# Queueing operations of four small chains one step later in a Fourier, gated and feed-forward kernel

## The chip, the cores and the metric

The kernel runs on one core of a Trainium2 chip. The engines of the core work side by side, each through its own queue in order: TensorE (PE in the profile; PEld is its load of weights), VectorE (DVE), ScalarE (ACT), GpSimd (POOL) and SyncE (SP), which here only issues DMAs. The metric is the device time of one execution in microseconds.

## The reference

Three parts follow one another over `x` of 4 x 3072 x 256:

```python
X = np.fft.rfft(x, axis=1)
Yr = Xr @ w_r - Xi @ w_i + b_r
Yi = Xr @ w_i + Xi @ w_r + b_i
Yr = np.sign(Yr) * np.maximum(np.abs(Yr) - 0.01, 0.0)   # and Yi alike: the soft threshold
x = np.fft.irfft(Yr + 1j * Yi, n=3072, axis=1)

xk = mu_k * x + (1.0 - mu_k) * x_prev                   # x_prev: one token earlier
xr = mu_r * x + (1.0 - mu_r) * x_prev
k = np.maximum(xk @ w_k, 0.0)                           # 256 -> 1024
x = sigmoid(xr @ w_r) * (k * k @ w_v)                   # 1024 -> 256

h = x @ w_in                                            # 256 -> 2048
g = h * np.clip(h + 3.0, 0.0, 6.0) / 6.0
out = g @ w_out                                         # 2048 -> 256
```

The weights of the second and third part come as 64-bit floats.

## The kernel before

Every product is made of three matmuls on fp32r pairs (`three`, L150): high by high, low by high, high by low. The pair of a value is made by `split` (L145): ACT rounds it into the high part, DVE subtracts that for the low part. So nearly each matmul waits for a chain that goes from ACT to DVE.

PE, ACT, DVE and POOL run in the order in which the program emits their instructions (`manual_schedule`, L228); no scheduler moves them. Generators lay the order out: a `yield` ends a *step*, and the loops at the end call the steps of several generators in turn. DMAs are issued from SP in emission order too, the tables of the transforms from POOL.

**The transforms.** The Fourier transform of a batch has a first stage (`s1`, 8 steps per batch, through `sc_a` in DRAM), a middle (`mid`, 12 pairs of groups, through `sc_b`) and an end (`ib`, 8 steps, into `sc_y`). A step of `mid` holds `s2` (12 matmuls, and the split `Xh`, `Xl`), then `mix` (24 matmuls with `w_r` and `w_i`, the bias added at L361, the soft threshold in L362 and L363, on DVE), and `ia` (6 matmuls), whose inputs `yh`, `yl` are split by `split_y` (L366) one step after. `ends` holds the last two pairs of `mid`.

**The weights' decode.** `Weights.load` brings 128x512 64-bit floats from DRAM; `decode` (L184) makes an fp32 value of the two 32-bit halves. L196 takes the exponent out on DVE, L197 and L198 build the power of two on ACT, L200 to L202 put sign and mantissa together on DVE, L204 multiplies, L210 splits. `decoder` (L212) runs jobs staggered: a new job each second step, and on each step one further step of each running job, so three jobs stand at different points of the chain. Buffers for the loaded halves come in threes (`stw`, `stt`).

**The order of the stages.** `first` (L451) is batch 0's transform as far as two `ib` steps, with the decode of `wr`, `wk`, `wv` on the steps named in `DECODE` (L33). Then come 24 tiles of 512 tokens of the second part, five units each (L834): `r`, then `k` four times; the product with `w_v` (`u_v`) follows two units later. At each half unit a slot lets `ahead` (L862) make a step of `prep` for the next tile: `xf` on ACT, `xf` on DVE, the split `kh`, `kl`, twice over (for `xk` and `xr`). Between these units stand the steps of `later` (L453), the transforms of the rest (`feed`), until they run out at some 795 us; from there on the decode of `w_in` and `w_out` (`jobs2`, 16 jobs, 36 decoder steps) takes their place (`decode_to`, L855).

**The third part** runs over 24 tiles with 8 units each (L922). Tile 0 uses plain products (`u_i`, L593). In its units 3 to 7 `beside` also makes the sums of the weights (`sums`, L616, in four quarters c0 to c3) and of tile 1's tokens (`split_s`, L648) that Strassen's products want; tiles 1 to 23 use these (`u_s`, L682), and what is left of the sums (`aside`) goes into tile 1's units. The output product of a unit (`u_o`, 24 matmuls) is issued two units later, in three parts between the matmuls of `u_s` (`cut`, L696). Before the first `u_s` the PSUM pool of the stages before is closed and another one opened (L949).

Of the kernel before, what the change touches and what calls it, by code (L numbers as in the profile page):

```python
# [103 lines left out]
def fourier_mix_ffn_kernel(  # L104
# [54 lines left out]
    class Weights:  # L159
# [24 lines left out]
        def decode(self, staged, k, q, c, m):  # L184
            w, t = staged
            yield
            hi, lo = self.hi[:, k : k + q, c : c + m], self.lo[:, k : k + q, c : c + m]
            if self.wide:
                w = w.rearrange("p k (n s) -> p k n s", s=2)
                low, high = w[:, :, :, 0], w[:, :, :, 1]  # L190
                a = t[:, 0].rearrange("p (k n) -> p k n", k=q)
                f = t[:, 1].rearrange("p (k n) -> p k n", k=q)
                ai, au = a.bitcast(I32), a.bitcast(U32)
                ts, stt = nc.vector.tensor_scalar, nc.vector.scalar_tensor_tensor

                ts(au, high, 20, 0x7FF, op0=ALU.logical_shift_right, op1=ALU.bitwise_and)  # L196
                nc.scalar.activation(f, ai, AF.Relu, bias=top[:, 0], scale=-1.0)  # L197
                nc.scalar.activation(ai, f, AF.Relu, bias=top[:, 1], scale=-(2.0**23))  # L198
                yield
                stt(au, high, 0x80000000, au, op0=ALU.bitwise_and, op1=ALU.bitwise_or)  # L200
                ts(high, high, 0xFFFFF, 0x100000, op0=ALU.bitwise_and, op1=ALU.bitwise_or)
                stt(f, low, 2.0**-32, high, op0=ALU.mult, op1=ALU.add)  # L202
                yield
                nc.vector.tensor_mul(f, f, a)  # L204
            else:
                f = w
                yield
                yield
            yield
            split(f, hi, lo)  # L210

    def decoder(jobs, stage):  # L212

        running = []
        for n in range(2 * len(jobs) + 4):
            for r in running:
                next(r, None)
            running = running[-3:]
            if n % 2 == 0 and n // 2 < len(jobs):
                w, *job = jobs[n // 2]  # L220
                running.append(w.decode(w.load(stage, *job), *job))
            yield
# [5 lines left out]
    with tc.manual_schedule(engines=order):  # L228
# [7 lines left out]
        omu = cst.tile([128, 2, 2], F32, name="omu")  # L236
        half = cst.tile([128, 1], F32, name="half")
        top = cst.tile([128, 2, 1], F32, name="top")
        bias = fp.tile([128, 3, D], F32, name="bias")
# [38 lines left out]
        def fetch():  # L278

            split_chunks(head["use"] + 4)  # L280
            load_chunks(head["split"] + 4)
# [31 lines left out]
        def mid(b):  # L313
# [31 lines left out]
            def mix(j):  # L345
# [13 lines left out]
                yl = fp.tile([128, 512], F32R, tag="yl", bufs=2, name="yl")  # L359
                bs = bias[:, 0:2] if j == 0 else bias[:, 1:3]  # L360
                nc.vector.tensor_add(y, p[:, 0:512], bs.rearrange("p g d -> p (g d)"))  # L361
                nc.vector.tensor_scalar(m, y, LAM, 0.0, op0=ALU.add, op1=ALU.min)  # L362
                nc.vector.scalar_tensor_tensor(y, y, LAM, m, op0=ALU.subtract, op1=ALU.max)  # L363
                yy[j] = (y, yh, yl)

            def split_y(j):  # L366
# [3 lines left out]
            def ia(j):  # L370
# [8 lines left out]
                nc.sync.dma_start(out=gb[j], in_=sb[:, 0:2])  # L379

            for j in range(NP + 1):
                if j < NP:
                    s2(j)
                load_t(b, j + 2)
                if j >= 2:
                    split_y(j - 2)
                if j < NP:
                    yield
                if j:
                    mix(j - 1)  # L390
                    fetch()
                    yield
                if 2 <= j < NP:
                    ia(j - 2)

            def end(j):
# [70 lines left out]
        nc.vector.memset(zero, 0.0)  # L467
        nc.vector.memset(half, 0.5)
        nc.vector.memset(top[:, 0], 1170.0)
        nc.vector.memset(top[:, 1], 254 * 2.0**23)  # L470

        def vectors():
# [4 lines left out]
            with nc.allow_non_contiguous_dma(reason="two vectors"):  # L477
                for i, m in enumerate((mu_k, mu_r)):
                    nc.sync.dma_start(out=mus[:, i], in_=m.rearrange("(a p) -> p a", p=128))
            nc.vector.tensor_scalar(omu, mus, -1.0, 1.0, op0=ALU.mult, op1=ALU.add)  # L480


# [9 lines left out]
        def prep(i):  # L492
# [9 lines left out]
            for w in (1, 0):  # L502
# [13 lines left out]
                l = kb.tile([128, 2, TOK], F32R, tag="kl", bufs=3, name="kl")  # L516
                nc.scalar.activation(h, xf, AF.Copy)  # L517
                nc.vector.tensor_sub(l, xf, h.bitcast(F32))  # L518
                xs[i, w] = h, l
# [72 lines left out]

        def u_i(i, j):  # L593
            xh, xl = xt[i]
# [11 lines left out]
            nc.vector.scalar_tensor_tensor(g, g, 1.0, p, op0=ALU.min, op1=ALU.mult)  # L606
            split(g, h, l)
            hg[i, j] = (h, l)
# [73 lines left out]
        def u_s(sp, pz, i, j, other, before, aside):  # L682
# [12 lines left out]
            c11, c21 = cc[:, 0:256], cc[:, 256:512]  # L695
            cut = [len(other) * n // 3 for n in range(4)]  # L696

# [130 lines left out]
        preps = prep(0)  # L828
        for _ in range(3):
            next(preps)  # L830
            next(preps)
            next(fs)

# [18 lines left out]

        done2 = 0

        def decode_to(n):  # L855
# [6 lines left out]
        def ahead(i, slot):  # L862

            nonlocal preps
            if i + 1 == len(seq):
# [8 lines left out]
            if slot == late and i + 1 < len(seq):  # L874
                b, t = seq[i + 1]
                drain(b, (TOK * t + TOK - 1) // N1 // 4 if t else 0)
                load_y(i + 1)
                preps = prep(i + 1)
            elif slot >= late + 2:
                next(preps, None)  # L880

        for n, (i, kind, j) in enumerate(units):
# [19 lines left out]
            if not live_f:  # L902
                if jobs2 is None:
# [13 lines left out]
                    jobs2 = decoder(wi.jobs + wo.jobs, stage2)  # L917
                decode_to(36 * (n - n0 + 1) // (len(units) - n0))
        units = [(i, j) for i in range(len(tiles)) for j in range(8)]
        pend = []  # L920
        before = []
        for n, (i, j) in enumerate(units):  # L922
            if i == 0:
                decode_to(max(done2 + 2, 2 * (j // 2 * 2 + 1) + 6, 2 * (8 + j) + 6))
                u_i(i, j)
                if lag:
# [3 lines left out]
                elif j > 2:  # L930
                    for f in u_o(*pend.pop(0)):
                        f()
                if j == 3:
                    decode_to(len(wi.jobs + wo.jobs) * 2 + 4)
                    stage.close()
                    sp = ctx.enter_context(tc.tile_pool(name="sp", bufs=1))
                    sw = [sp.tile([128, 4, 8, 128], F32R, name=f"sw{c}") for c in range(2)]
                    c0, c1, c2, c3 = (sums(sp, c) for c in range(4))
                    x1 = split_s(sp, 1)
                    beside = {3: c0[:2], 4: c0[2:] + c1[:1], 5: c1[1:], 6: x1[:2], 7: x1[2:] + c2[:1]}  # L940
                    aside = c2[1:] + c3
                if j >= 3:
                    for on_vector, on_scalar in beside[j]:
                        on_vector()
                        if on_scalar:
                            on_scalar()
            else:
# [38 lines left out]
```

## Time and profile before

| | us |
|---|---|
| median of three runs | 2081.03 (2080.89 to 2084.46) |
| the profiled execution | 2082.47 |
| its span | 2080.7 |
| PE busy | 1992.8 (96%) |
| PE's weight loads busy | 1844.5 (89%) |
| DVE busy | 1549.8 (74%) |
| ACT busy | 1323.2 (64%) |

The granted clock of TensorE was 0.976 of full speed over the span. A busy time says in how much of the span an engine worked on something; the stages differ, so the stretches between the stages' borders are read one by one. 0 to 40 us is the first stage of batch 0, 40 to 125 its middle, 125 to 195 the rest of `first` and the first tile's start, 195 to 795 the second part beside the transforms, 795 to 1052 the second part beside the decode, 1052 to 1120 tile 0 of the third part and the passage to tile 1, and 1120 to the end the Strassen tiles.

### The profile page before, as it was taken

The page shows a single profiled execution, that of the slowest core. Times are in us where ns is not written, and L with a number is a line of the kernel's source. Part 1 is how long each engine was busy: PE and PEld are TensorE (multiplying, and loading weights), DVE is VectorE, ACT ScalarE, POOL GpSimd, SP SyncE. Part 2 cuts the span into 40 slices and gives each one's busy share as a digit, 9 for nine tenths or more (in the row PEclk, how much of TensorE's full clock was granted, in tenths as well). Part 3 has the DMA queues.
Part 4 walks back from the last instruction along what each step waited for, and adds up shares of the span by engine and source line. Part 5 has one row for each costly group of instructions (what it writes and reads, how often), then busy time and mean ns, then how long its engine had stood idle before and what let it go on. Part 6 is the DMA issues. An engine that isn't in the chain of part 4 may idle for free.

```text
span 2080.7 us, 33798 instructions
## 1 busy us (share of the span) xinstructions
PE 1992.8 (96%) x13928; PEld 1844.5 (89%) x13928; DVE 1549.8 (74%) x1975; ACT 1323.2 (64%) x1917; POOL 35.0 (2%) x63
## 2 busy tenths in 40 slices
PE   6878999999999999889998999999999999999998
PEld 4867998898789888667787999999999999999998
DVE  3868667777677686767777777877787778777875
ACT  5556447555754565555646777777777777667775
POOL 0000000000000000000000000000000000000000
PEclk7978999999999999999999999999999999999999
DMA  9765447543653352122100001100110011001100
GB/s 265 240 205 165 123 114 228 163 142 115 216 170 111 95 179 65 63 75 77 51 31 24 29 23 29 32 21 23 30 32 21 22 31 32 21 22 31 32 11 21
DMA packets 106988, 175.85 MB, mean 85 GB/s; under 512 B 12945, under 2 KB 63314, under 8 KB 106834
## 3 DMA queue, kind: packets, MB, share of 16 engines
q1 hardware_dynamic: 96034, 141.76, 22.1%
q0 software_dynamic: 10480, 31.67, 5.7%
q8 instruction: 109, 1.79, 0.4%
q14 instruction: 45, 0.37, 0.1%
q10 hardware_dynamic: 320, 0.26, 0.0%
HBM read 110.35 MB, written 63.31 MB: 83 GB/s over the span
## 4 chain that ended last, share of the span: by engine, by line
PE 76%; DVE 14%; ACT 6%; issue 2%; DMA 2%; SPq 0%; ACTq 0%; DVEq 0%
PE oacc L776 24%; PE rq L776 15%; PE acc L156 8%; PE pk L156 7%; PE cc L776 6%; PE mix L156 5%; PE s L156 4%; DVE g L552 2%; DVE gl L553 2%; PE pr L156 2%; DVE xf L511 1%; PE ia L156 1%; DVE kl L518 1%; PE ib L421 1%; PE ib L420 1%
## 5 line engine op out<-in xcount | busy, mean ns | idle before, releaser
L776 PE MATMUL oacc<-wo_hi,gl 128*128 128x256 f32 x1536 | 426.7, 278 | 0.6 <-DVE gl L750 0.6
L776 PE MATMUL oacc<-wo_hi,gh 128*128 128x256 f32 x1536 | 427.1, 278 | 0.0
L776 PE MATMUL oacc<-wo_lo,gh 128*128 128x256 f32 x1536 | 425.4, 277 | 0.0
L776 PEld LDWEIGHTS oacc<-wo_hi,gl 128*128 128x128 f32 x1536 | 288.7, 188 | 1.0 <-DVE gl L750 0.8
L776 PEld LDWEIGHTS oacc<-wo_hi,gh 128*128 128x128 f32 x1536 | 288.5, 188 | 0.2
L776 PEld LDWEIGHTS oacc<-wo_lo,gh 128*128 128x128 f32 x1536 | 288.7, 188 | 0.0
L732 DVE TENSOR_TENSOR c<-rq,s 128x512 f32<-128x512 f32 x184 | 127.3, 692 | 184.2 <-ACT s L728 184.2
L745 DVE SCALAR_TENSOR_TENSOR g<-g,c 128x1024 f32<-128x1024 f32 x184 | 225.5, 1226 | 27.1 <-ACT g L744 17.4
L749 ACT ACTIVATE gh<-g 128x1024 fp32r<-128x1024 f32 x184 | 195.2, 1061 | 55.8 <-DVE g L745 55.8
L750 DVE TENSOR_TENSOR gl<-g,gh 128x1024 fp32r<-128x1024 f32 x184 | 223.7, 1216 | 1.2 <-ACT gh L749 1.2
L776 PE MATMUL rq<-th,sw 128*128 128x256 f32 x1104 | 217.4, 277 | 7.3 <-DVE g L606 7.3
L744 ACT ACTIVATE g<-c,half 128x1024 f32<-128x1024 f32 x184 | 211.5, 1150 | 4.1 <-DVE c L733 1.4
L712 ACT ACTIVATE s<-rq 128x512 f32<-128x512 f32 x184 | 109.9, 598 | 112.0 <-PE rq L776 111.5
L776 PEld LDWEIGHTS rq<-th,sw 128*128 128x128 f32 x1104 | 166.4, 188 | 7.5 <-DVE g L606 7.5
L156 PE MATMUL acc<-gl,wv_hi 128*128 128x512 f32 x384 | 153.8, 400 | 13.3 <-DVE gl L553 13.3
L547 ACT ACTIVATE g<-pk 128x1024 f32<-128x1024 f32 x96 | 97.6, 1016 | 106.5 <-PE pk L156 106.4
L156 PE MATMUL pk<-kh,wk_hi 128*128 128x512 f32 x384 | 152.8, 398 | 9.3 <-ACT kh L517 5.2
L776 PE MATMUL rq<-tl,sw 128*128 128x256 f32 x552 | 153.9, 279 | 2.8 <-DVE tl L679 2.8
L148 DVE TENSOR_TENSOR al<-a,ah 96x512 fp32r<-96x512 f32 (+1 forms) x176 | 114.9, 684 | 55.2 <-ACT ah L147 55.2
L156 PE MATMUL acc<-gh,wv_hi 128*128 128x512 f32 x384 | 153.2, 399 | 1.6 <-ACT gh L551 1.5
L156 PE MATMUL acc<-gh,wv_lo 128*128 128x512 f32 x384 | 152.2, 396 | 0.0
L156 PE MATMUL pk<-kl,wk_hi 128*128 128x512 f32 x384 | 151.9, 396 | 0.0
(150 smaller groups left out, 4953.0 us busy)
## 6 DMA issues: line engine op xcount, KB each, us to landing
tt<-in_tab_dram POOLq DMA_DIRECT2D x40, 640.0 KB, 4.9
yt<-sc_y SPq DMA_DIRECT2D x23, 608.0 KB, 3.9
a<-in_x_dram SPq DMA_DIRECT2D x64, 192.0 KB, 3.5
sc_a<-s1sb SPq DMA_DIRECT2D x32, 384.0 KB, 3.9
a<-sc_a SPq DMA_DIRECT2D x48, 256.0 KB, 3.2
sc_b<-iasb SPq DMA_DIRECT2D x48, 256.0 KB, 4.8
a<-sc_b SPq DMA_DIRECT2D x64, 192.0 KB, 3.1
sc_y<-ysb SPq DMA_DIRECT2D x32, 384.0 KB, 2.9
```

The costliest lines, as they stand in the source:

```text
L148: nc.vector.tensor_sub(l, src, h.bitcast(F32))
L156: nc.tensor.matmul(o, a, c, start=first and i == 0, stop=last and i == n - 1, **kw)
L547: nc.scalar.activation(g, p, AF.Relu)
L552: nc.vector.tensor_mul(g, g, g)
L553: nc.vector.tensor_sub(l, g, h.bitcast(F32))
L712: nc.scalar.activation(s[:, 1:3].rearrange("p a n -> p (a n)"), rq, AF.Copy)
L732: nc.vector.tensor_add(c[:, 1::2], two(rq), s[:, 0:2])
L744: nc.scalar.activation(g, c, AF.Relu, bias=half, scale=1.0 / 6.0)
L745: nc.vector.scalar_tensor_tensor(g, g, 1.0, c, op0=ALU.min, op1=ALU.mult)
L749: lambda: nc.scalar.activation(h, g, AF.Copy),
L750: lambda: nc.vector.tensor_sub(l, g, h.bitcast(F32)),
L776: return lambda: nc.tensor.matmul(o, lhs, rhs, start=start, stop=stop, skip_group_check=True)
```

## The change

Four chains are cut at other places into steps; three of them keep their instructions.

- *Decode.* The `yield` stands after L196 instead of after L198, L204 follows L202 without one, and the two halves of the split at L210 are steps of their own. A job takes six steps behind its load instead of five, and `decoder` runs one step more.
- *Tiles' inputs.* In `prep` the low part `kl` is a step of its own, eight steps instead of six per tile. `ahead` spreads those that are left over the slots that are left, and the loop ahead of the units makes all eight for tile 0.
- *Soft threshold.* `bias` is lowered by `LAM` once (768 columns, on DVE, in `vectors`). `mix` is a generator now: it adds the bias, then after `fetch` an activation on ACT makes relu(-y - 2 `LAM`) with the column `lam2` as its bias, and at the top of the next pair DVE takes the maximum of y and minus that. The operation at L362 goes.
- *Sums and tile 0.* Tile 1's sums (`x1`) come first, from unit 3 on, and what `u_i` gets as `between` is emitted between the unit's rounding copy and its low part. c0 and c1 up to its rounding copy stay in tile 0; c1's low part, all of c2 and c3 go to tile 1 (`aside`). The decode is finished ahead of `u_i` of unit 3, not behind it, and the first `u_s` issues all of `u_o`'s 24 matmuls ahead of its own.

```diff
@@ Weights.decode
                 ts(au, high, 20, 0x7FF, op0=ALU.logical_shift_right, op1=ALU.bitwise_and)
+                yield
                 nc.scalar.activation(f, ai, AF.Relu, bias=top[:, 0], scale=-1.0)
                 nc.scalar.activation(ai, f, AF.Relu, bias=top[:, 1], scale=-(2.0**23))
                 yield
...
                 stt(f, low, 2.0**-32, high, op0=ALU.mult, op1=ALU.add)
-                yield
                 nc.vector.tensor_mul(f, f, a)
...
             yield
-            split(f, hi, lo)
+            nc.scalar.activation(hi, f, AF.Copy)
+            yield
+            nc.vector.tensor_sub(lo, f, hi.bitcast(F32))
@@ decoder
-        for n in range(2 * len(jobs) + 4):
+        for n in range(2 * len(jobs) + 5):
@@ mix
                 nc.vector.tensor_add(y, p[:, 0:512], bs.rearrange("p g d -> p (g d)"))
-                nc.vector.tensor_scalar(m, y, LAM, 0.0, op0=ALU.add, op1=ALU.min)
-                nc.vector.scalar_tensor_tensor(y, y, LAM, m, op0=ALU.subtract, op1=ALU.max)
                 yy[j] = (y, yh, yl)
+                yield
+                nc.scalar.activation(m, y, AF.Relu, bias=lam2, scale=-1.0)
+                yield
+                nc.vector.scalar_tensor_tensor(y, m, -1.0, y, op0=ALU.mult, op1=ALU.max)
@@ mid
+            rest = iter(())
             for j in range(NP + 1):
+                next(rest, None)
                 if j < NP:
                     s2(j)
...
                 if j:
-                    mix(j - 1)
+                    rest = mix(j - 1)
+                    next(rest)
                     fetch()
+                    next(rest)
                     yield
...
+            next(rest, None)
@@ constants and vectors
+        nc.vector.memset(lam2, -2 * LAM)
...
+            nc.vector.tensor_scalar(bias, bias, LAM, None, op0=ALU.subtract)
@@ prep
                 nc.scalar.activation(h, xf, AF.Copy)
+                yield
                 nc.vector.tensor_sub(l, xf, h.bitcast(F32))
@@ u_i
-            split(g, h, l)
+            nc.scalar.activation(h, g, AF.Copy)
+            for f in between:
+                f()
+            nc.vector.tensor_sub(l, g, h.bitcast(F32))
@@ u_s
-            cut = [len(other) * n // 3 for n in range(4)]
+            cut = [len(other) * n // 3 for n in range(4)] if (i, j) > (1, 0) else [0, 0, 0, 0]
+            if (i, j) == (1, 0):
+                for f in other:
+                    f()
@@ before the units' loop
-        for _ in range(3):
+        for n in range(4):
             next(preps)
             next(preps)
-            next(fs)
+            if n < 3:
+                next(fs)
@@ ahead
                 preps = prep(i + 1)
+                left = 8
             elif slot >= late + 2:
-                next(preps, None)
+                for _ in range(-(-left // (10 - slot))):
+                    next(preps, None)
+                    left -= 1
@@ the second part's loop
-                decode_to(max(done2 + 2, 2 * (j // 2 * 2 + 1) + 6, 2 * (8 + j) + 6))
-                u_i(i, j)
+                decode_to(max(done2 + 2, 2 * (j // 2 * 2 + 1) + 7, 2 * (8 + j) + 7))
+                if j == 3:
+                    decode_to(len(wi.jobs + wo.jobs) * 2 + 5)
...
+                    x1 = split_s(sp, 1)
+
+                    beside = {
+                        3: ([x1[0][0]], [x1[0][1]]),
+                        4: ([x1[1][0]], [x1[1][1], c0[0][0]]),
+                        5: ([x1[2][0]], [c0[1][0]]),
+                        6: ([c1[0][0]], [c0[1][1], c0[2][0]]),
+                        7: ([c1[1][0]], [c1[1][1]]),
+                    }
+                    both = lambda f, g: lambda: (f(), g())
+                    aside = [(both(c1[2][0], c2[0][0]), None), c2[1], (both(c2[2][0], c3[0][0]), None)] + c3[1:]
+                u_i(i, j, beside[j][0] if j >= 3 else ())
                 if lag:
...
-                if j == 3:
-                    decode_to(len(wi.jobs + wo.jobs) * 2 + 4)
...
-                    beside = {3: c0[:2], 4: c0[2:] + c1[:1], 5: c1[1:], 6: x1[:2], 7: x1[2:] + c2[:1]}
-                    aside = c2[1:] + c3
                 if j >= 3:
-                    for on_vector, on_scalar in beside[j]:
-                        on_vector()
-                        if on_scalar:
-                            on_scalar()
+                    for f in beside[j][1]:
+                        f()
```

## Rows read from the trace of the kernel before

**Rows 1.** Windows by stage: stretch, us, busy us (instructions) of PE, PEld, DVE, ACT, POOL, PEclk, DMA, GB/s.
```profile
40.00:125.00 85.00, 71.31 (x522) 67.15 (x522) 69.44 (x114) 44.15 (x72) 8.63 (x14) 0.92 0.76 230
125.00:195.00 70.00, 54.86 (x244) 46.06 (x245) 47.92 (x80) 48.90 (x84) 0.56 (x2) 0.68 0.59 182
195.00:795.00 600.00, 595.47 (x3515) 524.09 (x3514) 432.90 (x564) 347.37 (x494) 22.44 (x39) 0.99 0.49 149
795.00:1052.00 257.00, 235.60 (x997) 187.97 (x996) 195.95 (x240) 152.53 (x183) 0.00 (x0) 0.98 0.21 68
1052.00:1120.00 68.00, 57.91 (x362) 52.38 (x361) 45.50 (x64) 29.02 (x34) 0.00 (x0) 0.92 0.07 21
1120.00:2081.00 961.00, 955.19 (x8234) 954.79 (x8232) 744.79 (x893) 680.00 (x1025) 0.00 (x0) 1.00 0.09 26
...
60.00:116.00 56.00, 48.12 (x384) 45.88 (x385) 51.29 (x84) 31.70 (x52) 6.15 (x10) 1.00 0.71 219
...
1105.00:1110.00 5.00, 5.00 (x32) 5.00 (x33) 2.73 (x8) 0.98 (x2) 0.00 (x0) 0.72 0.00 0
```

**Rows 2.** Waits of PE, 795 to 1052 (releaser: us in total, times, longest).
```profile
PE acc L156 <- DVE gl L553: 13.3, 14, 2.0
```

**Rows 3.** Timeline around 842 us: start, us, instruction, idle before and releaser.
```profile
838.88 0.72 ACT L197 ACTIVATE stt<-stt,top 128x512 f32<-128x512 int32 x1 [4.64 <-DVE stt L196]
...
843.48 1.23 DVE L552 TENSOR_TENSOR g<-g 128x1024 f32<-128x1024 f32 x1 [3.43 <-ACT gh L551]
...
846.02 0.50 PE L156 MATMUL acc<-gl,wv_hi 128*128 128x512 f32 x1 [1.79 <-DVE gl L553]
```

**Rows 4.** Waits of ACT and DVE, 795 to 1052.
```profile
ACT stt L197 <- DVE stt L196: 67.3, 16, 6.2
DVE g L552 <- ACT gh L551: 30.0, 12, 3.6
```

**Rows 5.** Groups by line and shape, whole span: busy us, mean ns, idle before.
```profile
L362 DVE TENSOR_SCALAR ym<-yf 128x512 f32<-128x512 f32 x48 | 20.6, 428 | 1.6
...
L197 ACT ACTIVATE stt<-stt,top 128x512 f32<-128x512 int32 x25 | 18.1, 724 | 91.8 <-DVE stt L196 91.8
...
L202 DVE SCALAR_TENSOR_TENSOR stt<-stw 128x512 f32<-128x512 uint32 x25 | 17.3, 693 | 0.9
...
L196 DVE TENSOR_SCALAR stt<-stw 128x512 uint32<-128x512 uint32 x25 | 10.5, 420 | 0.0
```

**Rows 6.** Chain of waits at 177 and 896 us: start, us, piece.
```profile
177.50 5.47 PE pk L156 x12
...
184.73 2.74 PE pk L156 x12
...
896.01 4.23 PE pk L156 x10
```

**Rows 7.** Timeline of 125 to 195 us.
```profile
127.52 0.80 PE L156 MATMUL ia<-yh,tt 128*128 128x256 f32 x2 [4.49 <-ACT yh L147]
...
160.47 0.53 PE L420 MATMUL ib<-fi,ah 96*128 96x192 f32 x1 [2.43 <-DVE ysb L425]
...
175.06 0.72 ACT L197 ACTIVATE stt<-stt,top 128x512 f32<-128x512 int32 x1 [3.81 <-DVE stt L196]
...
177.50 0.80 PE L156 MATMUL pk<-kh,wk_hi 128*128 128x512 f32 x1 [3.73 <-ACT g L547]
```

**Rows 8.** Waits of PE, 40 to 125 us.
```profile
PE ia L156 <- DVE yl L148: 8.6, 11, 2.0
```

**Rows 9.** Timeline at 43 us, the first step of the middle transform.
```profile
43.57 0.42 PE L156 MATMUL s<-tt,al 128*128 128x64 f32 x1 [2.39 <-DVE al L148]
```

**Rows 10.** Timeline of 1097 to 1106 us, from tile 0 to tile 1.
```profile
1098.02 1.06 ACT L678 ACTIVATE th<-xs 128x1024 fp32r<-128x1024 f32 x1 [1.93 <-DVE xs L664]
...
1101.38 0.79 PE L776 MATMUL rq<-th,sw 128*128 128x256 f32 x2 [7.34 <-DVE g L606]
...
1104.93 0.58 PE L776 MATMUL rq<-tl,sw 128*128 128x256 f32 x1 [2.75 <-DVE tl L679]
```

More of the change, by code (lines that the diff above doesn't have):

```diff
@@ L237, in fourier_mix_ffn_kernel @@
         half = cst.tile([128, 1], F32, name="half")
+        lam2 = cst.tile([128, 1], F32, name="lam2")
         top = cst.tile([128, 2, 1], F32, name="top")
@@ L591, in split_2, with u_i @@
             xt[i] = (h, l)
-        def u_i(i, j):
+        def u_i(i, j, between=()):
             xh, xl = xt[i]
@@ L853, in fourier_mix_ffn_kernel @@
         done2 = 0
+        left = 0
         def decode_to(n):
@@ L862, in ahead @@
         def ahead(i, slot):
-            nonlocal preps
+            nonlocal preps, left
             if i + 1 == len(seq):
@@ L917, in fourier_mix_ffn_kernel @@
                     jobs2 = decoder(wi.jobs + wo.jobs, stage2)
-                decode_to(36 * (n - n0 + 1) // (len(units) - n0))
+                decode_to(37 * (n - n0 + 1) // (len(units) - n0))
         units = [(i, j) for i in range(len(tiles)) for j in range(8)]
@@ L923, in fourier_mix_ffn_kernel @@
             if i == 0:
-                decode_to(max(done2 + 2, 2 * (j // 2 * 2 + 1) + 6, 2 * (8 + j) + 6))
-                u_i(i, j)
+                decode_to(max(done2 + 2, 2 * (j // 2 * 2 + 1) + 7, 2 * (8 + j) + 7))
+                if j == 3:
+                    decode_to(len(wi.jobs + wo.jobs) * 2 + 5)
+                    stage.close()
+                    sp = ctx.enter_context(tc.tile_pool(name="sp", bufs=1))
+                    sw = [sp.tile([128, 4, 8, 128], F32R, name=f"sw{c}") for c in range(2)]
+                    c0, c1, c2, c3 = (sums(sp, c) for c in range(4))
+                    x1 = split_s(sp, 1)
[9 more added lines that the diff above has]
+                u_i(i, j, beside[j][0] if j >= 3 else ())
                 if lag:
@@ L932, in fourier_mix_ffn_kernel @@
                         f()
-                if j == 3:
-                    decode_to(len(wi.jobs + wo.jobs) * 2 + 4)
[L935 to L939, printed above, removed]
-                    beside = {3: c0[:2], 4: c0[2:] + c1[:1], 5: c1[1:], 6: x1[:2], 7: x1[2:] + c2[:1]}
-                    aside = c2[1:] + c3
                 if j >= 3:
-                    for on_vector, on_scalar in beside[j]:
-                        on_vector()
-                        if on_scalar:
-                            on_scalar()
+                    for f in beside[j][1]:
+                        f()
             else:
```

## The prediction

> **What bounds the kernel now.** I read the windows by stage first, because the engines' busy shares over the whole span mix stages with different limits. The stage from 1120 us to the end is nearly half the time, and there the weight load of TensorE is busy 954.8 of 961.0 us with the granted clock at 1.00 [rows 1]. Nothing that an order of instructions on VectorE (DVE) or ScalarE (ACT) does can shorten it, as long as it adds no wait. From 195 to 795 us TensorE is busy 595.5 of 600.0 us, so at most 4.5 us lie there. What can be won is the idle time of the other stages: 85.0 - 71.3 = 13.7 us in 40 to 125, 70.0 - 54.9 = 15.1 in 125 to 195, 257.0 - 235.6 = 21.4 in 795 to 1052, 68.0 - 57.9 = 10.1 in 1052 to 1120, together 60.3 us, and the matmuls that ran after such gaps at half clock (mean clock 0.68 to 0.98 in these rows).
>
> Next I asked who ends TensorE's waits. In 795 to 1052 it is the low part of the squared activation 14 times, 13.3 us [rows 2]. The timeline of one such place shows why [rows 3]: ACT stands 4.64 us in front of the decode's first activation (L197), waiting for the exponent that L196 takes out; the evictions queued behind it come late; DVE then stands 3.43 us for `gh`; and TensorE stands 1.79 us for `gl`. VectorE itself was never short of time. Grouped: ACT waits 67.3 us in 16 such places, DVE 30.0 us in 12 for the answer [rows 4]. DVE is busy 196.0 of 257.0 us in this stage (76%), ACT 152.5 (59%). So the bound there is order, two in-order queues standing in front of each other.
>
> **The change part by part.** Times are against the profiled execution: span 2080.7, the execution 2082.47 us. The median of the three runs is 2081.03, 1.44 lower; I take the sum off that.
>
> *Decode.* Each job's five cross-engine steps become six. No instruction is added. On even decoder steps all is now DVE: the low part of one job (like L202, 693 ns), then L200, L201, L202, L204 of the next, then L196 of a third. With four operations near 0.69 and two near 0.43 that is 3.6 us [rows 5]. On odd steps all is ACT: one rounding copy and two activations of 724 ns. Before, the even step held 1.1 us of DVE and the pair of activations right behind it. So L197 finds its input made one decoder step earlier and the 4.64 us wait has no cause. What is late next is the 3.6 us block of DVE: behind it stand the square and the low part of the next unit. Between a unit's evictions and TensorE's use of them lie four groups of 12 matmuls, each 2.74 us at full clock [rows 6], which covers one block, but DVE's share rises to 196.0/236 = 83% once the idle time is gone, so some waits will remain. The weight loads on SP keep their order and get one step less margin for their buffer (three buffers, two steps between the last read and the load).
>
> *Tiles' inputs.* The low part goes one step behind its rounding copy, and eight steps are spread over the free slots. It takes away the waits of `kl` for `kh`, and the drain of the last steps at the start of the next tile. In the four of 24 tiles where fewer than eight slots are free, two steps share a slot and the old wait stays there.
>
> The two together own the 21.4 us of 795 to 1052 and 2.0 us more: ten matmuls ran in 4.23 us there, at the half-clock level, where 12 take 2.74 [rows 6], 4.23 - 10 x 0.228 = 1.95. Ends: 9 us if the blocks keep more than half, 23.4 if nothing is left. I take 18.5, nearer the upper end because the waiting engine (ACT) is the one with room.
>
> In 125 to 195 the same two edits meet three places [rows 7]. TensorE's wait of 3.73 us at 177.50 stands behind L197's wait of 3.81 us; after it 12 matmuls took 5.47 instead of 2.74 us [rows 6]. That is 3.73 + 2.73 = 6.5 us; I take 5.0 (ends 2.0 and 6.5), for DVE's block then stands in front of the `ysb` sums. The wait of 2.43 us at 160.47 hangs on an `xf` scaling that stood in ACT's queue for `kl`; the new order puts an `ib` unit between them: 2.0 (ends 0 and 2.4). The wait of 4.49 us at 127.52 is for `yh`, behind the activations of one decode step; the step is now a DVE block in front of the soft threshold's last operation, which gives most of it back: 1.2 (ends 0 and 4.5). The smaller waits of this window: 0.5 (ends 0 and 1.5). The wait for the reload of `sc_b` stays.
>
> *Soft threshold.* In each of the 48 steps of the middle transforms L362 (428 ns, DVE) goes and one activation with a column bias comes (like L197, 724 ns, ACT). From 60 to 116 us DVE sets the pace: it is busy 51.3 of 56.0 us [rows 1], and from 40 to 125 TensorE waits 11 times, 8.6 us, for `yl` [rows 8]. At 42 matmuls a step, 384 matmuls are 9.1 steps, 12.2 us for two. Twelve operations of 0.43 us less on DVE would be 5.1 us. But of two steps one now has the DVE block of 3.6 us, and the threshold is a round trip: `yl` 0.69, block 3.6, add 0.69, activation 0.72, maximum 0.69, and `Xl` of 768 columns, 1.0 by L202's rate, are 7.4 us, some 0.5 less where starts overlap. The step without the block is TensorE's, 42 matmuls of about 0.12 us, 5.0. Both make 11.9 us where now 12.2 stand, 0.3 on each of five pairs: I take 1.0 gained (ends -2.0 and 8.6). The new subtraction on the bias stands in DVE's queue in front of the first `al`, for which TensorE waits 2.39 us at 43.57 [rows 9]: an operation of L362's kind on 768 columns, an estimate of 0.43 to 0.69 us, taken as 0.6 lost. In 195 to 795 two groups of 2.74 us run beside each step and cover the longer chain: 0 (ends -4.0 and 4.5).
>
> A 128x512 activation with a column bias takes 724 ns where the DVE operation took 428 [rows 5]. [...]
>
> *Weight sums and tile 0.* The gaps of 7.34 and 2.75 us at 1101.38 and 1104.93 [rows 10] end with the release of tile 0's last PSUM pair and with `tl`. ACT stood 1.93 us in front of `th`, and the eviction of the last unit was queued behind. Now `tl` is made two units earlier, sums fill DVE's wait for `gh`, one sum and one low part move into tile 1, and the first Strassen unit issues 24 ready matmuls of tile 0 ahead of its own. The work moved to tile 1, four sums of 256 columns and one low part of 1024, is at most 4 x 0.42 + 2 x 0.69 = 3.1 us; it falls into units of some 45 matmuls in which DVE is busy 744.8 of 961.0 us [rows 1], and into the first of them, where no gate of an earlier unit is due. After the gap TensorE did 32 matmuls in 5 us [rows 1] where the later stage does one in 955.2/8234 = 0.116 us: 11 x 0.116 = 1.3 us lost to the clock's half level. 10.1 + 1.3 - 0.4 (the first unit has no foreign matmuls between its own to cover ACT's copies) = 11.0 (ends 8.0 and 11.4).
>
> **Sum.** 18.5 + 5.0 + 2.0 + 1.2 + 0.5 + 1.0 - 0.6 + 0 + 11.0 = 38.6 us. 2082.47 - 38.6 = 2043.9 for the execution, 2081.03 - 38.6 = 2042.4 for the median.
>
> **The rivals.** *The block becomes the wait.* If each of 16 blocks leaves TensorE as long a wait as the 14 of now, 13.3/14 = 0.95 us, 15.2 us stay in 795 to 1052 and 8.2 are won instead of 18.5: 2053. For it: 83% on DVE. Against it: the four groups of matmuls between eviction and use.
>
> *More comes back.* All 23.4 us there and all 8.6 in 40 to 125: 2042.4 - 4.9 - 7.6 = 2030. For it: DVE loses 5.1 us where it sets the pace. Against it: the round trip.
>
> *ACT's longer operation counts.* All 48 x 0.296 = 14.2 us on the path: 2057. Against it: ACT is busy 347.4 of 600.0 us in 195 to 795 [rows 1]. [...]
>
> *Slower.* The threshold's round trip comes late at the inverse transform. If activation and maximum (0.72 + 0.69 = 1.42 us) stand uncovered in all 48 steps, 68 us are added: 2110. It decides from 38.6/48 = 0.8 us a step. For it: TensorE does wait for `yl` in 40 to 125, about 0.8 us each time [rows 8]. Against it: from 195 to 795 no wait of TensorE is for `yl`; the idle 4.5 us there are too few.
>
> *Nothing moves.* DVE is more than one decoder step behind, so that L197 waits all the same: 2081.
>
> **How the numbers follow.** Forecast 0.60 (own range 2034 to 2051), block 0.16, more 0.11, ACT 0.03, slower 0.05, nothing 0.05. The range of 2027 to 2061 holds the first four and leaves out the last two, 0.1, and the tails of the others. A difference under 0.2%, 4.2 us, counts as none, about what a measurement of this kernel can tell: faster 0.90, same 0.05, slower 0.05.
>
> **What would show it.** Right: L197 no longer waits for L196; TensorE's idle time in the decode stage falls from 21.4 to some 4 us; the gap at tile 0's end and the one at 177 us are gone; from 1120 us on the pace per matmul is the same. Wrong: waits of TensorE for `gl` with DVE busy without a break before them (the block), or new waits for `yl` between 195 and 795 us (the round trip).

## The result and the profile after

The changed kernel takes 2103.72 us (2102.93 to 2109.72) against 2081.39: ratio 1.011, interval 1.0089 to 1.0131. I had forecast 2042.4 with a range of 2027 to 2061, so it went the other way, by +22 us instead of -39. The profiled execution has a span of 2101.2 us (2080.7 before).

The windows of the changed kernel, same stretches and columns as [rows 1], the last two cut to its own stages:

```profile
40.00:125.00 85.00, 71.78 (x521) 69.22 (x522) 63.12 (x100) 50.17 (x83) 7.92 (x14) 0.89 0.73 222
125.00:195.00 70.00, 58.02 (x275) 48.97 (x274) 55.76 (x90) 53.11 (x89) 1.81 (x4) 0.76 0.69 216
195.00:795.00 600.00, 597.01 (x3521) 524.52 (x3520) 415.02 (x527) 372.60 (x530) 21.39 (x37) 0.99 0.48 147
795.00:1052.00 257.00, 223.06 (x909) 179.31 (x908) 183.10 (x224) 139.72 (x170) 0.00 (x0) 0.93 0.21 65
...
760.50:1064.80 304.30, 270.36 (x1116) 218.38 (x1116) 215.66 (x259) 165.87 (x200) 0.00 (x0) 0.94 0.21 67
1120.00:2100.00 980.00, 976.18 (x8252) 975.38 (x8250) 748.03 (x896) 680.40 (x1028) 0.00 (x0) 1.00 0.09 25
```

Windows at fixed times cut different work out of two kernels. So I read the same points of the program in both timelines: the first `pr` matmul of tile 0 and of tile 15, by when only tiles and decode are left, the first `pi` matmul (tile 0 of the third part), and the last matmul.

| us | first `pr` | to tile 15's `pr` | to first `pi` | to the last matmul |
|---|---|---|---|---|
| before | 162.3 | 638.4 | 251.6 | 1023.5 |
| after | 159.9 | 633.2 | 271.7 | 1031.8 |
| change | -2.4 | -5.2 | +20.1 | +8.3 |

So in these two profiles the kernel gains 7.6 us up to tile 15, loses 20.1 in the decode stage where I had forecast a gain of 18.5, and loses 8.3 behind it where I had forecast a gain of 11.0. There are two losses, and the experiments show that each comes and goes without the other.

**The decode stage.** The waits of PE between 760.5 and 1064.8 us in the changed kernel are all of these two lines:

```profile
PE pk L156 <- DVE kl L532: 32.4, 9, 4.0
PE acc L156 <- DVE gl L567: 1.6, 2, 1.3
```

The waits for `gl` [rows 2] are gone but for 1.6 us. In their place TensorE waits once in each of the nine tiles from 15 to 23 for `kl`, the low part of that tile's own input, which is made while the tile before runs. The same stretch of the program (768.1 to 1052.2 us) stands so in the windows of the kernel before:

```profile
768.10:1052.20 284.10, 262.70 (x1117) 210.35 (x1116) 212.53 (x258) 166.30 (x199) 0.00 (x0) 0.98 0.22 72
```

With the same matmuls, TensorE is idle 33.9 us instead of 21.4, and busy 270.4 instead of 262.7, with a mean granted clock of 0.94 instead of 0.98: 12.5 and 7.7 make the 20.2 us between the two stretches. The chain of waits of the changed kernel at one of the nine places (start, us, piece):

```profile
846.18 1.15 DVE kl L532
847.32 0.02 issue
847.35 1.34 ACT xf L519 x2
848.68 0.96 ACT gh L565
849.64 0.02 issue
849.67 1.24 DVE g L566
850.90 0.02 issue
850.92 1.23 DVE gl L567
852.15 1.32 DVE xf L524 x2
853.47 0.60 DVE wi_lo L212
854.08 0.61 DVE stt L201
...
856.60 0.34 DVE stt L196
856.93 1.15 DVE g L566
...
859.31 1.23 DVE kl L532
860.54 0.04 issue
860.59 3.92 PE pk L156 x10
```

The chain of a tile's second input starts at 847.35 only when the first input's `kl` has been made, because both use the one buffer `xf`; its own `kl` then stands on the tile's last slot, behind the decode's block (853.5 to 856.9), the unit's square and its low part. TensorE needed it 3.92 us before it came (timeline of the changed kernel):

```profile
860.59 0.50 PE L156 MATMUL pk<-kl,wk_hi 128*128 128x512 f32 x1 [3.92 <-DVE kl L532]
```

**From 1120 us on** TensorE is as busy as before, at the same granted clock of 1.00, but a matmul takes 976.2/8252 = 0.1183 us where it took 955.2/8234 = 0.1160 [rows 1]. In the inner stretch of 1200 to 2000 us the windows of the kernel before and of the changed one show it without the ends:

```profile
1200.00:2000.00 800.00, 800.00 (x6898) 800.00 (x6898) 624.20 (x747) 571.46 (x864) 0.00 (x0) 1.00 0.10 26
```

```profile
1200.00:2000.00 800.00, 800.00 (x6769) 800.00 (x6768) 614.01 (x736) 560.40 (x847) 0.00 (x0) 1.00 0.09 26
```

0.1160 against 0.1182 us per matmul, evenly over the stage (848 or 849 matmuls in each 100 us, against 864); for 8250 of them 18 us. With the 9.9 us that the edit of tile 0 wins, that makes the 8.3 lost. No wait stands behind it: the profile has none of PE in these 800 us, in either kernel. The one thing of the diff that reaches these tiles is `lam2`: a tile of one column takes 32 bytes per partition in the program's allocation, which puts kb, kw and sp behind it 32 bytes higher (`gh` at 18240 instead of 18208), while w2, which is laid from the other end, stays.

### The profile page after: what moved, and what is told of

Read it like the earlier page. It is cut to its first block, busy times and chain, and to the rows that moved or that the text cites. A ratio compares the mean times of both kernels' runs of the same rounds, so it can differ in the third digit from the quotient of the medians.

```text
span 2101.2 us, 33830 instructions
## 1 busy us (share of the span) xinstructions
PE 2016.1 (96%) x13928; PEld 1869.2 (89%) x13928; DVE 1530.8 (73%) x1929; ACT 1351.5 (64%) x1965; POOL 34.5 (2%) x63
## 4 chain that ended last, share of the span: by engine, by line
PE 79%; DVE 11%; ACT 5%; DMA 2%; issue 2%; SPq 0%; ACTq 0%; DVEq 0%
PE oacc L799 25%; PE rq L799 15%; PE acc L156 9%; PE pk L156 8%; PE cc L799 6%; PE mix L156 6%; PE s L156 4%; DVE g L566 2%; DVE gl L567 2%; PE pr L156 2%; PE ia L156 1%; ACT gh L565 1%; DVE xf L524 1%; PE ib L432 1%; DVE kl L532 1%
## 5 line engine op out<-in xcount | busy, mean ns | idle before, releaser
L799 PE MATMUL oacc<-wo_lo,gh 128*128 128x256 f32 x1536 | 431.0, 281 | 0.0
L156 PE MATMUL pk<-kl,wk_hi 128*128 128x512 f32 x384 | 156.6, 408 | 32.4 <-DVE kl L532 32.4
L566 DVE TENSOR_TENSOR g<-g 128x1024 f32<-128x1024 f32 x96 | 117.4, 1223 | 93.8 <-ACT gh L565 93.7
L156 PE MATMUL pk<-kh,wk_lo 128*128 128x512 f32 x384 | 153.8, 400 | 0.0
```

The costliest lines, as they stand in the source:

```text
L156: nc.tensor.matmul(o, a, c, start=first and i == 0, stop=last and i == n - 1, **kw)
L566: nc.vector.tensor_mul(g, g, g)
L799: return lambda: nc.tensor.matmul(o, lhs, rhs, start=start, stop=stop, skip_group_check=True)
```

## The experiments

All were timed beside the kernel before (2081.1 to 2082.1 us in the four groups of runs); each has a name, given in brackets.

**Two causes told apart.** The shift without the change (before_32):

```diff
         half = cst.tile([128, 1], F32, name="half")
+        spare0 = cst.tile([128, 1], F32, name="spare0")
```

> The kernel before with one unused column of 32 bytes per partition behind `half`, which moves the buffers of kb, kw and sp up by 32 bytes, as `lam2` does in the changed kernel; no instruction differs. Theory (place of the buffers): from 1120 us on a matmul takes 0.1183 us instead of 0.1160, as in the changed kernel, some 8,250 matmuls, +19 us: 2100. Rival (the order of work around the first Strassen unit sets another phase between the engines, which lasts): nothing changes, 2081.

Measured: 2104.36 us, ratio 1.0108 (1.0092 to 1.0125), and 6769 matmuls in 1200 to 2000 us, as many as in the changed kernel. Up to the first `pi` it runs as the kernel before (1050.2 us against 1052.2). An unused column costs as much as the whole change.

The change without the shift (after_noshift):

```diff
-        half = cst.tile([128, 1], F32, name="half")
-        lam2 = cst.tile([128, 1], F32, name="lam2")
+        half = cst.tile([128, 2], F32, name="half")
+        half, lam2 = half[:, 0:1], half[:, 1:2]
```

> The changed kernel with `lam2` as a second column of the tile of `half`, so that all buffers lie where they lay before; the instructions are the same. Theory (place): 2103.7 - 19 = 2085, with 0.1160 us per matmul from 1120 us on. Rival (order): 2104, with 0.1183.

Measured: 2084.94 us, ratio 1.0011 (1.0002 to 1.0021); windows:

```profile
1200.00:2000.00 800.00, 800.00 (x6899) 800.00 (x6898) 624.39 (x748) 572.44 (x864) 0.00 (x0) 1.00 0.10 26
```

The pace is that of before, and the 32.4 us of waits for `kl` are still there. The order of work around the first Strassen unit is out as a cause.

**The slot of `kl`.** On that kernel (after_slot8):

```diff
-                for _ in range(-(-left // (10 - slot))):
+                for _ in range(-(-left // max(1, 9 - slot))):
```

> The run above with the eight steps of the tiles' inputs spread so that the last (kl) falls on slot 8, one slot earlier. Theory (the nine waits for kl, 32.4 us, come from the slot of the last step): they go, and with them most of the 7.7 us that the matmuls lost to the clock: 2085 - 35 to 40 = 2045 to 2050. Rival (the block of decode operations on VectorE is the cause, whatever the slot): the wait is shorter by the half unit or turns up for gl, 2070 to 2085.

Measured: 2045.29 us, ratio 0.9818 (0.9803 to 0.9833). In the waits of PE between 770 and 1040 us one line is left:

```profile
PE acc L156 <- DVE gl L567: 2.2, 1, 2.2
```

Half a unit earlier takes all nine waits away, and from tile 15 to the first `pi` it is 224.9 us. Up to tile 15, though, its profile needs 800.4 us where that of after_noshift needed 787.6. So the next edit keeps slot 9 beside the transforms (after_slot8_late):

```diff
-                for _ in range(-(-left // max(1, 9 - slot))):
+                for _ in range(-(-left // max(1, (10 if live_f else 9) - slot))):
```

> As after_slot8, but the last step of the tiles' inputs falls on slot 8 only once the transforms have run out; beside them it stays on slot 9 as in the changed kernel. Up to the first unit of tile 15 the profile of after_slot8 needed 800.4 us, that of after_noshift 787.6. Theory (doubling a step in the first slot of each tile stands in front of the transforms' own operations there): most of those 12.8 us come back, 2045 - 10 = 2035. Rival (the two profiles differ there by how the DMAs and the clock fell in that one execution): 2045.

Measured: 2038.08 us, ratio 0.9786 (0.9770 to 0.9802): 7.2 us under after_slot8, nearer the theory than the rival. Its profile has 793.5 us up to tile 15, so part of the 12.8 us was how one execution fell. This kernel is the fastest of the ones tried.

**The parts one by one**, each put alone into the kernel before, the buffers where they lay. The decode (decode_alone; its counts of steps, one higher, are left out here):

```diff
                 ts(au, high, 20, 0x7FF, op0=ALU.logical_shift_right, op1=ALU.bitwise_and)
+                yield
...
-                yield
                 nc.vector.tensor_mul(f, f, a)
...
-            split(f, hi, lo)
+            nc.scalar.activation(hi, f, AF.Copy)
+            yield
+            nc.vector.tensor_sub(lo, f, hi.bitcast(F32))
```

> The kernel before with the decode's edit alone (its own counts of steps with it); tiles' inputs, threshold and tile 0 as before. Theory (L197's wait for L196 made TensorE's waits for gl, and the block of decode operations costs nothing): the 14 waits for gl, 13.3 us, and the half clock behind some of them go, one or two waits for the tiles' inputs stay: 2081 - 17 to 22 = 2059 to 2064. Rival (the edit needs the low part kl to step back as well, since kl stands in front of the decode's block and waits for kh): half of it, 2070. Second rival (the block itself delays gl): 2078 to 2085.

Measured: 2056.65 us, ratio 0.9874 (0.9860 to 0.9889), a gain of 25.4 us. Waits of PE, 770 to 1040 us:

```profile
PE pk L156 <- DVE kl L520: 2.8, 1, 2.8
PE pk L156 <- ACT kh L519: 2.0, 1, 2.0
PE acc L156 <- DVE gl L555: 0.6, 3, 0.3
```

From tile 15 to the first `pi` it takes 228.9 us, 22.7 less than before. It beats the theory's range, and both rivals fall: the block costs nothing that shows, and `kl` did not have to move.

The tiles' inputs (prep_alone):

```diff
                 nc.scalar.activation(h, xf, AF.Copy)
+                yield
                 nc.vector.tensor_sub(l, xf, h.bitcast(F32))
...
-                next(preps, None)
+                for _ in range(-(-left // (10 - slot))):
+                    next(preps, None)
+                    left -= 1
```

> The kernel before with the edit of the tiles' inputs alone (eight steps, the last on slot 9); the decode as before. Theory (the slot decides: the first product of a tile needs kl half a unit behind slot 9, whatever stands in the decode): waits of pk for kl of 2 to 4 us in nine tiles between 800 and 1052 us, beside the old waits for gl: 2081 + 15 to 30 = 2096 to 2111. Rival (only the decode's new block makes kl late): 2081, within 4 us.

Measured: 2117.74 us, ratio 1.0176 (1.0161 to 1.0191), a loss of 36.1 us, more than the upper end. Waits of PE, 790 to 1090 us:

```profile
PE pk L156 <- DVE kl L519: 35.7, 9, 4.2
PE acc L156 <- DVE gl L554: 6.7, 7, 1.7
PE pk L156 <- ACT kh L517: 5.5, 3, 1.9
```

The nine waits come with the old decode too, so it is the slot and not the new block.

The sums and tile 0 (tile0_alone; an extract of the edit):

```diff
-                u_i(i, j)
+                u_i(i, j, beside[j][0] if j >= 3 else ())
...
-                    for on_vector, on_scalar in beside[j]:
+                    for f in beside[j][1]:
...
```

> The kernel before with the edit of the sums, tile 0 and the first Strassen unit alone. By the profiles the stretch from tile 0's first matmul to the last one is 1013.6 us in after_noshift and 1023.5 before, so theory: 2081 - 10 = 2071. Rival (the gap closed only because the decode, which runs into tile 0, was cut anew as well): a gap of 3 to 7 us stays, 2075 to 2079.

Measured: 2069.74 us, ratio 0.9937 (0.9922 to 0.9951), a gain of 12.3 us. From the first `pi` to the last matmul it takes 1013.5 us instead of 1023.5; the rival falls.

The soft threshold (thresh_alone; an extract of the edit):

```diff
-                nc.vector.tensor_scalar(m, y, LAM, 0.0, op0=ALU.add, op1=ALU.min)
-                nc.vector.scalar_tensor_tensor(y, y, LAM, m, op0=ALU.subtract, op1=ALU.max)
...
+                nc.scalar.activation(m, y, AF.Relu, bias=lam2, scale=-1.0)
+                yield
+                nc.vector.scalar_tensor_tensor(y, m, -1.0, y, op0=ALU.mult, op1=ALU.max)
```

> The kernel before with the soft threshold's edit alone, `lam2` as a second column of the tile of `half`. Theory (round trip against less VectorE work in the first batch's middle, nothing elsewhere): 2081, within 2 us. Rival (VectorE sets the pace from 60 to 116 us and has 5.1 us less): 2076. Rival on the other side (five waits of mix for the maximum, 8.3 us in the profile of after_noshift, are new): 2086.

Measured: 2083.80 us, ratio 1.0008 (0.9999 to 1.0018). No difference that can be told, as the theory had it; the faster rival falls, and 1.7 us is less than the slower one's 5. Of the waits of PE in 40 to 125 us, the 8.6 us of [rows 8] became the first, second and fourth of these lines, 9.3 us together; the 2.9 us answer to [rows 9]:

```profile
PE mix L156 <- DVE yf L362: 3.6, 4, 0.9
PE ia L156 <- DVE yl L148: 3.2, 9, 0.6
PE s L156 <- DVE al L148: 2.9, 1, 2.9
PE ia L156 <- ACT yh L147: 2.5, 5, 1.2
```

L362 is in this kernel the addition of the bias, which reads the result of the `mix` before; it is not the maximum, as the expectation has it.

The changed kernel without the edit of the tiles' inputs, the buffers where they lay before (after_prep_undone):

> The changed kernel without the edit of the tiles' inputs, buffers where they lay before: decode, threshold and tile 0. From the runs of single parts, 2081.7 - 25.4 - 12.3 + 1.7 = 2045.7. If the parts add up, 2044 to 2048; if the edit of the tiles' inputs is what brings the first 800 us down to 793 in after_slot8_late, 2038 is not reached; rival (with the maximum gone from VectorE, the old split does as well as the new): 2036 to 2041.

```diff
                 nc.scalar.activation(h, xf, AF.Copy)
-                yield
                 nc.vector.tensor_sub(l, xf, h.bitcast(F32))
...
-                for _ in range(-(-left // (10 - slot))):
-                    next(preps, None)
-                    left -= 1
+                next(preps, None)
```

Measured: 2047.41 us, ratio 0.9839 (0.9823 to 0.9855). The parts add up to within 2 us (2045.7), and the rival falls: the tiles' inputs in eight steps, on the right slot, bring 9.3 us more (2038.08).

**What about the place of the buffers.** The tiles from 1120 us on read three groups of buffers: kb (`gh`, `gl` and parts of the inputs) and sp (`sw`, `th`, `tl`), which are laid from the front, and w2 (the weights `wi` and `wo`), laid from the other end. Two columns at the front (before_64):

```diff
+        spare0 = cst.tile([128, 1], F32, name="spare0")
+        spare1 = cst.tile([128, 1], F32, name="spare1")
```

> The same with two unused columns, 64 bytes. If what counts is the place modulo 64 bytes, the time is that of the kernel before, 2081. If any shift against the output weights (whose place stays) costs, 2100. Rival (order): 2081 as well, so it tells only the two address readings apart.

Measured: 2102.97 us, ratio 1.0103 (1.0088 to 1.0118), 6744 matmuls in 1200 to 2000 us. The place modulo 64 bytes is not it.

A column behind kb (before_sp32):

```diff
+    gap = ctx.enter_context(tc.tile_pool(name="gap", bufs=1))
+    spare = gap.tile([128, 1], F32, name="spare")
     kw = ctx.enter_context(ExitStack())
```

> The kernel before with an unused column of 32 bytes between kb and the pools behind it: the sums (sw), th and tl move up by 32 bytes; gh, gl, xh4, xl4 (kb) and wi, wo (w2) stay. Reading A (how the two operands of a matmul lie to each other): of 45 matmuls of a unit the 24 of the output keep their operands' places, so at most half of the 19 us, 2083 to 2091. Reading B (the place of kb alone counts): 2081. Reading C (the place of sp alone): 2100.

Measured: 2094.19 us, ratio 1.0068 (1.0053 to 1.0083), 6830 matmuls. That is 3 us above reading A's range, and neither B nor C. The upper bound of A counted matmul by matmul, and that fails: from one output product to the next it is 0.1162 us on the mean in 1200 to 2000 us (0.1151 before), though `gh`, `gl` and `wo` lie to one another as before. So in this run the pace of a matmul does not hang on its own two operands alone.

A column at the other end (before_w2):

```diff
+        edge = ctx.enter_context(tc.tile_pool(name="edge", bufs=1, side="right"))
+        spare = edge.tile([128, 1], F32, name="spare")
         ff = ctx.enter_context(ExitStack())
```

> The kernel before with an unused column of 32 bytes at the other end of SBUF, so that wi and wo (and the transforms' buffers) move down by 32 bytes and kb and sp stay. Reading A: gh and gl against wo lie as far apart as with the column at the front, so most of the 19 us, 2092 to 2102. Reading B or C (the place of kb or sp as such): 2081.

Measured: 2104.48 us, ratio 1.0109 (1.0094 to 1.0124), 6735 matmuls. kb and sp lie where they lay, so B and C fall. It is 2.5 us above reading A's range, and equal to before_32 (2104.36), in which the three groups have the same distances to one another at other addresses.

One place less at the front (front_down):

```diff
-        half = cst.tile([128, 1], F32, name="half")
-        top = cst.tile([128, 2, 1], F32, name="top")
+        top = cst.tile([128, 3, 1], F32, name="top")
+        half = top[:, 2]
```

> The kernel before with `half` as a third column of the tile of `top`: one 32-byte place less at the front, so kb, kw and sp move down by 32 bytes; w2 stays. Reading A (how far apart the two operands of a matmul lie): another distance than before, slow as with the shifts up, 2093 to 2104. Rival (any place of the front buffers but the two or three tried ones is as good): 2081.

Measured: 2096.64 us, ratio 1.0074 (1.0059 to 1.0089), 6787 matmuls. Then both this and the column at the other end (all_down):

> The same with the unused column at the other end as well: kb, kw, sp and w2 all move down by 32 bytes, so each operand of the Strassen tiles and of the output lies as far from its partner as before. Reading A (distance): 2081. Reading D (the absolute place of either operand): 2093 to 2106, as with each shift by itself.

Measured: 2083.81 us, ratio 1.0009 (1.0000 to 1.0018); windows:

```profile
1200.00:2000.00 800.00, 800.00 (x6899) 800.00 (x6898) 623.16 (x745) 571.80 (x864) 0.00 (x0) 1.00 0.09 26
```

Two shifts that cost 15.5 and 22.8 us alone cost 2.7 us together, and the pace is that of before. So in these three runs the cost goes with the distance between the buffers, not with the address of any.

These runs leave open which engine's reads and writes have a part in it, for ScalarE and VectorE work on kb and sp too. The last output products of the program tell more, because during ten of them no other engine works and no DMA moves data. The first and the tenth of these in the kernel before, in before_32 and in after_noshift:

```profile
2073.23 0.28 PE L776 MATMUL oacc<-wo_hi,gh 128*128 128x256 f32 x1
...
2074.25 0.28 PE L776 MATMUL oacc<-wo_hi,gh 128*128 128x256 f32 x1
```

```profile
2090.92 0.28 PE L777 MATMUL oacc<-wo_hi,gh 128*128 128x256 f32 x1
...
2091.99 0.28 PE L777 MATMUL oacc<-wo_hi,gh 128*128 128x256 f32 x1
```

```profile
2072.65 0.28 PE L799 MATMUL oacc<-wo_hi,gh 128*128 128x256 f32 x1
...
2073.71 0.28 PE L799 MATMUL oacc<-wo_hi,gh 128*128 128x256 f32 x1
```

That is 0.113, 0.119 and 0.118 us each. So the slow pace does not need the other engines. But after_noshift has its buffers where the kernel before has them, and its row of 31 output products just ahead of these took 0.113 us each. The same distances allow both paces, then, and what sets one or the other at the start of a row is open; over the whole stage the paces of the two kernels are alike.

Four columns at the front (before_128):

> The kernel before with four unused columns, 128 bytes, at the front. If the distance counts modulo 128 bytes, 2081; if it counts modulo more, or as such, 2093 to 2104.

With four columns, 2100.16 us, ratio 1.0095 (1.0079 to 1.0112), 6769 matmuls: a distance 128 bytes off is no better. A longer period was not tried.

## Why the prediction was wrong

The sum failed at two of its steps. Of the 61.3 us between forecast and result, 18.8 are the place of the buffers (2103.72 to 2084.94) and 39.7 the slot of `kl` (2084.94 to 2045.29). Without these two the kernel takes 2045.29 or, with slot 9 kept beside the transforms, 2038.08.

*Tiles' inputs.* "It takes away the waits of `kl` for `kh`, and the drain of the last steps at the start of the next tile." I counted what the move took away and never asked when the moved part is needed. This put a gain where the runs have a loss: 36.1 us by itself, nine waits of up to 4.2 us. Six steps from slot 2 end on slot 7; eight end on slot 9, one unit later, and the first `k` unit of the next tile reads that `kl` with two groups of 12 matmuls between (2.74 us each [rows 6]). With 5.5 us of cover and the unit's own square, its low part and the decode's block on VectorE ahead, that was to be worked out from the rows I had. None of my rivals was this wait: the block's rival put it on `gl`, at 8.2 us won; the slower one put its 68 us on the threshold. From 195 to 795 us the transforms' matmuls lengthen a unit and hide the later slot: no wait of PE for `kl` stands there in the changed kernel.

*"From 1120 us on the pace per matmul is the same."* I took it that only an added wait could lengthen this stage ("Nothing that an order of instructions [...] does can shorten it, as long as it adds no wait"). The constant `lam2`, which stands in the sum at nothing, moved the buffers and cost 18.8 us at the same number of waits, none.

The other steps held in direction, but for the threshold; in size only tile 0 did. That 2045.29 lies so near the forecast of 2042.4 is in part luck: the decode stage gave 8.2 us more than forecast, and the stretch up to tile 15 next to nothing in that profile.

- *Decode.* L197's wait of 67.3 us [rows 4] is gone, the waits for `gl` with it; what ACT still waits in the decode is 18.5 us in nine places, for L204 ahead of the rounding copy. 18.5 us were forecast for decode and inputs in this stage; decode alone takes 22.7 off and with the inputs on slot 8 it is 26.7 (251.6 to 224.9). The block of 3.6 us costs next to nothing in this stage, so my top end of 23.4 was too low.
- *125 to 195 us.* The 3.73 us at 177.50 [rows 7] are 0.83 now, the 4.49 at 127.52 are 2.30, the 2.43 for `ysb` at 160.47 are gone but for 0.22, and 2.18 us for `ysb` at another place are new, behind the decode's block, the price that I had taken off the first. In the changed kernel's timeline:

```profile
127.87 0.80 PE L156 MATMUL ia<-yh,tt 128*128 128x256 f32 x2 [2.30 <-ACT yh L147]
...
180.73 0.36 PE L431 MATMUL ib<-fi,ah 96*128 96x192 f32 x1 [2.18 <-DVE ysb L436]
```

 Up to tile 15, 9.1 us were forecast (all terms but decode stage and tile 0); the profiles show 7.6, and 7.1 in after_slot8_late, but 0.2 in after_slot8. One profile cannot give this size: nine kernels whose order is that of before as far as tile 15 reach it between 797.6 and 805.1 us, the two with the order of the changed kernel at 793.1 and 787.6. A gain is seen, its size is not.
- *Soft threshold.* VectorE was freed, but another wait took it back, and it is not my round trip. In the changed kernel's timeline `mix` waits for L365, the addition of the bias to the result of the `mix` before, which stands behind the decode's block (60.36 to 63.30 us) on VectorE:

```profile
63.22 0.68 DVE L365 TENSOR_TENSOR yf<-mix,bias 128x512 f32<-128x512 f32 x1
...
63.95 0.39 PE L156 MATMUL mix<-aw_hi,Xh 128*128 128x256 f32 x1 [1.40 <-DVE yf L365]
```

 The same wait stands four pairs of steps on at 114.96 us, so two steps take (114.96 - 63.95)/4 = 12.75 us, not the 11.9 of my estimate; before it was 12.00 (the wait for `yl` at 61.51 and, four pairs on, at 109.51), not the 12.2 that I had worked out. Taken as 0.4 gained net, measured 1.7 lost, and no change lies within the interval. The price of 14 us that a rival of mine put on the path for ScalarE's longer operation (724 ns against 428 [rows 5]) did not show: ScalarE's busy time rose from 347.4 to 372.6 us in 195 to 795, and all that TensorE waited there was 2.9 us for `ysb` on VectorE (4.5 before).
- *Tile 0.* Forecast 11.0; 9.9 by the profiles and 12.3 by the times. Of the gaps of 7.34 and 2.75 us [rows 10] this is left in the changed kernel:

```profile
1112.79 0.50 PE L799 MATMUL rq<-th,sw 128*128 128x256 f32 x2 [0.47 <-ACT s L746]
```

## What to carry to other kernels

When an operation is queued later, work out for each reader the slot at which it needs the result and what stands ahead on the producer's queue, not only which wait goes. An edit that also allocates something should be timed once with the allocation alone: here a column of 4 bytes and one step on the wrong slot, 18.8 and some 40 us, hid a change that is worth 2.1% without them. And parts of one idea are worth timing one by one: two of these four gain 25 and 12 us, one nothing, and one loses 36.

## What the runs showed of the hardware

From 1200 to 2000 us 128x256 matmuls, each with its own weight load, run back to back. With the buffers of the kernel before one takes 0.1160 us (800 us over 6898 matmuls), and as long with kb, kw, sp and w2 all moved by the same 32 bytes (all_down, 6899). In six other layouts, with five other sets of distances between kb, sp and w2, it takes 0.1171 to 0.1188 us (6830 to 6735 matmuls, one profile each), and the kernel 2094.19 to 2104.48 us instead of 2081.1 to 2082.1. The granted clock is 1.00 and TensorE busy for all of the 800.00 us in the kernel before, in all_down and, of the six, in before_32 (6769), so neither a lower clock nor a wait makes the difference between these. front_down and before_w2 cost 0.7 and 1.1% of this kernel, and the two shifts together (all_down), which restore the distances, 0.1%. That the slow pace does not need the other engines is shown only by the ten output products above (0.119 us each in before_32, 0.113 in the kernel before). What it is in the distance that counts, why a row at the distances of before can take either pace (0.113 and 0.118 us in after_noshift), and whether a better distance exists, stays open. From 195 to 795 us, where a matmul takes 600.0/3515 = 0.17 us on the mean [rows 1], no such loss shows: from tile 0's `pr` to tile 15's it is 638.4 us before and 635.3 in before_32, and 633.4 to 641.6 in all the shifted layouts.
